# A linear-attention and MLP kernel on one Trainium2 core: one group of small matrix products per unit instead of three, the MLP's block products in another order, and the whole instruction order written out anew

## The chip, the cores and the metric

The kernel runs on one core of one Trainium2 chip. The metric is device time in microseconds (us) of one execution; lower is better. All arithmetic is in 32-bit floats on the core's engines: PE (TensorE, matrix products; PEld is its loading of stationary operands), DVE (VectorE), ACT (ScalarE), POOL (GpSimd) and SP (SyncE, which only issues DMAs here). Each engine runs its own instructions in the order in which the program issues them, and waits at an instruction until what it needs is there. The order of the program text is therefore the order in each engine's queue.

## The reference

B=4 batches, H=8 heads, S=768 steps, D=48.

```python
f = 1.0 / (1.0 + np.exp(-f_logit))
for t in range(S):
    state = f[:, :, t, :, None] * state + einsum('bhd,bhe->bhde', k[:, :, t], v[:, :, t])
    y[:, :, t] = einsum('bhd,bhde->bhe', q[:, :, t], state)
x = y.transpose(0, 2, 1, 3).reshape(B, S, H * D)          # 4 x 768 x 384
xn = (x - mean(x)) / sqrt(var(x) + 1e-6) * g_ln
out = x + relu(xn @ w_ch1) @ w_ch2                         # 384 -> 1536 -> 384
```

## The kernel before, in words

The 768 steps are cut into 12 **units** of 64 steps. A unit holds the 4 batches and 8 heads of its steps, so 256 tokens of 384 numbers. A unit first goes through the attention part, then through the MLP part, and the program interleaves the attention of later units with the MLP of earlier ones.

**Attention of unit n** (function `attention`, a table of stages that are called by name). `gates` is the sigmoid; `after` and `upto` are running products of the gates (scans on DVE, L669 and L681); `k`, `q` and `kept` multiply keys, queries and the state by them. From unit 3 on (`DIRECT`) f, k, q and the scaled keys K are split into 16-bit planes on ACT (L440), stored to DRAM, and brought back transposed by a DMA on SP's queue (L455). Then come the small products, each in a quarter of the 128x128 array, 64 instructions to a kind (32 products; an fp32 product is two instructions):

- `carried` (L758): the queries times the state of the units before, into the PSUM tile `py`;
- `scores` (L772): keys times queries, into the PSUM tile `shared` (two banks);
- `causal` (L778): DVE copies the scores out of `shared` into `sc` through a mask, one instruction of 128x1024;
- `values` (L808): `sc` times v, added into `py`; ACT then copies `py` out as the unit's x (L819);
- `chunk` (L846): transposed keys `kt` times v, into `shared` again; `state` (L854, DVE) adds it to the kept state.

`stats` (L831 to L835: DVE, then POOL), `norm` (L876, DVE) and `turn` (L887: six PE transposes into `xp`; L889: six ACT multiplications into `xt`) make the transposed and normalized x.

**MLP of unit n.** For units 0 to 2 the first layer is plain. From unit 3 on, `by_blocks` computes it with 15 block products instead of 18 (L952, each 4 matmuls of 128x128x128 into one PSUM bank called bw, bx, bv, by or bz). Their left operands are blocks of `xt` or sums of them, `y`, which `sums_of_x` makes with nine DVE instructions (L922). Each product is then copied by ACT (L957) or added by DVE (L960) into `h`, and a relu by ACT (L963) follows. The second layer is plain for units 0 and 1 (L1027); from unit 2 on it is 7 products instead of 8 (L1046, each 6 matmuls of 128x192 output into one bank `pp`), from h and the sums s1 to s4 of its quarters (L931 to L934). DVE, POOL and ACT add them up (L1054), and `put` (L1059) sends the output.

**PSUM** has 8 banks: two for `shared`, two for `py`, and four that `one_bank` hands out in rotation to everything else (xp, bw to bz, pp, po, ph). A product that is handed a bank waits until the bank's former content has been read.

**The weights** arrive as 64-bit floats, in 12 pieces of 768 KB, and are fetched, read and rewritten as fp32 by the tokens `f`, `r` and `w`; the tokens `t`, `T`, `u`, `U` make the mixed weights of the second layer, `d` issues a matmul of nothing.

**Order.** A string of tokens gives the order of the whole program: `START` for the beginning, then `UNIT` for m = 3 to 11 with n=m+1, o=m+2, p=m+3, z=m+4. `m{m}` issues the next product of unit m's MLP, `a{n}.values` that stage of unit n's attention, `p`/`P` a split, `x` a transfer back, `l`/`L` a load, `s` and `y` the sums. So while unit m's MLP runs, its template issues 15 block products with the attention of unit n between them, and then the 7 products of the second layer.

**The fallback check.** `worst`, `pw`, `least_one` and `small` (L1141 to L1149) reduce the smallest running product of all units to one number. They are issued after units 9 and 10 of the template. At the end each engine loads that number into a register (L1154) and branches on it (L1155); the branch's other side is a general path that these inputs don't take.

Of the kernel before, what the change touches and what calls it, by code (L numbers as in the profile page):

```python
# [9 lines left out]
FP32 = mybir.dt.float32  # L10
# [291 lines left out]
START = """  # L302
d d L0f1 l0k1 a0.gates0 a0.carried a0.after0 d l0k0 d l0q0 a0.kx1 a0.upto0 a0.gates1 d f
l0q1 a0.after1 r a0.kx0 a0.k0 f a0.q0 a0.scores0 a0.upto1 L0v1 w a0.causal0 a0.k1 d l0v0
f r a0.q1 w a0.scores1 a0.values0 r a0.kt a0.causal1 f d a0.stats0 w a0.values1 d
a0.norm0 r a0.stats1 l1f w a0.chunk f a0.norm1 d a0.turn0 a1.gates h00 r h00 l1k
a1.after a0.turn1 a0.state h00 a1.upto l1q l1v h01 h01 f w h01 a1.q h00 l2q a1.kept f
h01 r a1.kx h01 a1.carried a1.k l2f a1.scores w r a1.kt h00 a1.causal a1.values f w l2k
a1.stats h00 f r a1.chunk a2.gates h01 a1.norm a1.turn l3f a2.kx f P3f0 m1 w r a2.after
a2.k p3f1 a2.upto a1.state r l3k f a2.kept m1 P3k1 w m1 m1 r w l2v m1 w p3k0 f m1 r x3f  # L310
a3.gates a2.q l3q m0 m0 a2.carried L4f a2.scores a2.kt w a2.causal x3k P3q1 m1 u T
a3.after U P3q0 L4k a2.values x3q a2.chunk U P4f1 m1 a3.k U a2.stats a2.norm P3K0 m0 m0
u a2.state P4k1 m0 u a2.turn P4k0 t p3K1 m0 m2 l4q p4f0 a3.upto l3v a3.kept u u p4q0
p4q1 m2 a3.q m2 u x4f u t l5f m1 a3.carried a3.scores m2 a4.gates m2 a3.causal m2 m1
a3.values a4.after x4k a3.kt s2 x4q P5f0 a4.k P5f1 a3.chunk u a3.stats a3.state L5k l5v
m2 a3.norm m1 p5k0 a4.upto l6f a4.q U p5k1 m1 x5f P4K1 l4v m2 m2 m2 U a3.turn l5q
a5.gates p4K0 y3 m2 a4.kept m2 m2
"""
UNIT = """
x{o}k a{n}.carried a{n}.scores p{p}f1 m{m} a{o}.after m{m} m{m} a{n}.kt a{n}.causal  # L320
p{o}q1 m{m} p{p}f0 m{m} m{m} m{m} a{n}.values m{m} P{o}q0 a{o}.upto m{m} l{p}k m{m}
a{n}.stats m{m} m{m} m{m} m{m} a{n}.norm m{m} a{n}.chunk a{n}.turn a{o}.k s{m} m{m}
p{p}k1 x{o}q a{n}.state L{z}f m{m} a{o}.q P{p}k0 m{m} p{o}K0 x{p}f y{n} l{p}q m{m}
a{o}.kept p{o}K1 a{p}.gates m{m} m{m} m{m} l{p}v
# [4 lines left out]
def kernel(  # L329
# [37 lines left out]
    FIRST = 3  # L367
    DIRECT = 3
# [135 lines left out]
    state = consts.tile([P, 2, GA, D], FP32)  # L504
    shared = two_banks("shared")
# [122 lines left out]
    x_of, norm_of, xn_of, xt_of, y_of, h_of, sums_of = {}, {}, {}, {}, {}, {}, {}  # L628
# [7 lines left out]
    def attention(n):  # L636
# [75 lines left out]
        def do_k(gs=both):  # L712
            kh = new("kh", [P, NS, T])
# [49 lines left out]
        def do_scores(gs=both):  # L763


            at["ps"] = ps = shared.rearrange("s r (e t) -> s r e t", t=T)
            kh, qh = at["kh"], at["qh"]
            for e, _ in of(gs):
                for b in range(2):
                    for r in range(2):  # L770
                        seg = 2 * e + b
                        nc.tensor.matmul(ps[half(b), r, e], lhsT=kh[head_rows(r), seg],  # L772
                                         rhs=qh[head_rows(r), seg], start=True, stop=True)

        def do_causal(gs=both):
            sc = new("sc", [P, 2, GA, T])
            if len(gs) == G:
                nc.vector.tensor_tensor(  # L778
                    out=sc.rearrange("s r e t -> s (r e) t"),
                    in0=at["ps"].rearrange("s r e t -> s (r e) t"),  # L780
# [4 lines left out]
                out=sc[:, :, es], in0=at["ps"][:, :, es], op=ALU.mult,  # L785
# [17 lines left out]
        def do_values(gs=both):  # L803
# [8 lines left out]
            if n not in x_of:  # L812
                x_of[n] = xs.tile([P, G, DM], FP32, tag="x", name=f"x{n}")
# [65 lines left out]
    def turn(n, gs):  # L879
        xn = xn_of[n]  # L880
        if n not in xt_of:
            xt_of[n] = work.tile([P, KD, W], FP32, tag="xt", bufs=2, name=f"xt{n}")
        xt = xt_of[n]
# [7 lines left out]

    def first_half(n, g):
        xt = xt_of[n]
# [294 lines left out]
```

## Time and profile before

| | |
|---|---|
| device times of three runs | 443.1, 441.15, 441.22 us; median 441.22 |
| span of the profiled execution (first to last instruction) | 435.1 us |
| median time less that span | 6.1 us |
| busy share of the span: PE, DVE, ACT, POOL | 96%, 77%, 50%, 26% |
| mean granted TensorE clock | 0.988 of full speed |
| last PE instruction ends, span ends | 430.7 us, 435.1 us |

The profile gives one span, and three times without saying which of them it belongs to; the median is set beside it here, so that about 6.1 us lie outside the span. A timeline row reads: start in us, duration in us, engine, line, operation, destination <- sources, size of the stationary operand, output shape, and the number of instructions run together; a bracket at its end is how long the engine was idle before it, and who released it. Matmuls are pipelined, so the durations of neighbouring rows overlap: what a group costs PE is read from the distance of its start to the next row's start.

### The profile page before, as it was taken

Reading aid. Unit: us, or ns where it says so; the run is one execution under the profiler, and the core shown is the slowest. Engines: PE = TensorE matmul, PEld = TensorE weight load, DVE = VectorE, ACT = ScalarE, POOL = GpSimd, SP = SyncE. Lnnn points to the kernel's source line nnn. Section 1 sums busy time; section 2 is a strip of 40 time slices with the busy share of each in tenths; the row PEclk is TensorE's granted clock in tenths of the full one; section 3 lists DMA queues with packets and bytes.
Section 4 is the critical chain, followed back from the end, with each engine's and each line's share of the span. In section 5 each row is a group of like instructions: output and inputs, shape, how many; then the busy total and the mean of one; then the engine's idle time right before and its main releaser. Section 6 shows DMA issues by size and latency. Waiting matters only on the chain.

```text
span 435.1 us, 12965 instructions
## 1 busy us (share of the span) xinstructions
PE 419.7 (96%) x5435; PEld 388.8 (89%) x5435; DVE 333.2 (77%) x539; ACT 217.2 (50%) x364; POOL 114.3 (26%) x148
## 2 busy tenths in 40 slices
PE   6699899999999999999999989999999999999995
PEld 4599787767879999999999989999999999999995
DVE  5999699669497698798798789699698599466361
ACT  2593876454253663663663664574564372260320
POOL 2351444932023214114114104104105003002021
PEclk9599999999999999999999999999999999999999
DMA  9998979958978787798798896998798781400101
GB/s 167 282 179 224 234 218 238 196 141 198 226 171 201 180 199 189 165 213 209 186 185 208 152 206 154 204 185 202 177 190 187 153 153 35 101 2 17 23 4 38
DMA packets 167647, 71.68 MB, mean 165 GB/s; under 512 B 151760, under 2 KB 157840, under 8 KB 167584
## 3 DMA queue, kind: packets, MB, share of 16 engines
q1 hardware_dynamic: 151728, 54.38, 62.3%
q0 software_dynamic: 3872, 12.64, 8.7%
q10 hardware_dynamic: 11984, 3.79, 4.1%
q8 instruction: 44, 0.72, 0.7%
q14 instruction: 19, 0.16, 0.1%
HBM read 28.31 MB, written 23.59 MB: 119 GB/s over the span
## 4 chain that ended last, share of the span: by engine, by line
PE 79%; DMA 6%; issue 5%; DVE 3%; ACT 2%; SPq 2%; POOL 1%; POOLq 0%; ACTq 0%
PE pp L1046 28%; PE bx L952 9%; PE ph L1017 7%; PE po L1027 7%; PE by L952 7%; PE bz L952 3%; PE ph L901 2%; PE py L758 2%; PE shared L772 2%; PE py L808 2%; PE bw L952 2%; DMA kt<-Khalves 2%; DMA w_0words<-in_moe_w_ch_dram 2%; PE shared L846 2%; PE xp L887 2%
## 5 line engine op out<-in xcount | busy, mean ns | idle before, releaser
L963 ACT ACTIVATE h<-h 128x512 f32<-128x512 f32 x45 | 28.1, 631 | 40.8 <-DVE h L960 35.3
L1046 PE MATMUL pp<-mixed,h 128*128 128x192 f32 x240 | 42.3, 326 | 0.0
L1046 PE MATMUL pp<-w,h 128*128 128x192 f32 x240 | 40.9, 327 | 0.0
L1046 PE MATMUL pp<-mixed,s 128*128 128x192 f32 x240 | 40.6, 326 | 0.0
L1046 PEld LDWEIGHTS pp<-mixed,h 128*128 128x128 f32 x240 | 39.5, 190 | 0.0
L1046 PEld LDWEIGHTS pp<-mixed,s 128*128 128x128 f32 x240 | 39.3, 190 | 0.0
L1046 PEld LDWEIGHTS pp<-w,h 128*128 128x128 f32 x240 | 38.8, 190 | 0.3
L960 DVE TENSOR_TENSOR h<-h,bx 128x512 f32<-128x512 f32 x27 | 18.4, 683 | 25.7 <-PE bx L952 23.7
L669 DVE TENSOR_TENSOR_SCAN after<-gates,ends 128x1040 f32<-128x1040 f32 (+1 forms) x13 | 30.4, 2340 | 8.0 <-ACT gates L696 4.6
L1027 PE MATMUL po<-w,h 128*128 128x384 f32 x96 | 32.2, 487 | 0.0
L1017 PE MATMUL ph<-xt,w 128*128 128x256 f32 x144 | 31.8, 380 | 0.2 <-ACT xt L889 0.2
L960 DVE TENSOR_TENSOR h<-h,by 128x512 f32<-128x512 f32 x36 | 24.7, 687 | 8.6 <-PE by L952 4.8
L1017 PEld LDWEIGHTS ph<-xt,w 128*128 128x128 f32 x144 | 27.2, 190 | 4.4 <-ACT xt L889 0.5
L952 PE MATMUL bx<-y,v 128*128 128x128 f32 x216 | 29.4, 279 | 0.0
L440 ACT COPY Kplanes<-kh 128x1024 uint16<-128x1024 uint16 x18 | 18.7, 1047 | 20.9 <-DMA khalves<-kplanes 20.9
L681 DVE TENSOR_TENSOR_SCAN upto<-gates,starts 128x1040 f32<-128x1040 f32 (+1 forms) x13 | 28.1, 2158 | 0.4
L1027 PEld LDWEIGHTS po<-w,h 128*128 128x128 f32 x96 | 17.9, 190 | 11.0
L1054 POOL TENSOR_TENSOR p1x<-p,x 128x192 f32<-128x192 f32 x10 | 9.5, 952 | 68.8 <-ACT p L1061 68.8
L952 PEld LDWEIGHTS bx<-y,v 128*128 128x128 f32 x216 | 26.2, 192 | 0.5
L957 ACT ACTIVATE h<-bw 128x512 f32<-128x512 f32 x9 | 5.4, 598 | 38.6 <-PE bw L952 38.6
L440 ACT COPY kplanes<-kraw 128x1024 uint16<-128x1024 uint16 x18 | 18.7, 1047 | 10.8 <-DMA fraw<-in_f_logit_dram 3.4
L834 POOL TENSOR_SCALAR rstd<-mv 128x2 f32<-128x2 f32 (+1 forms) x13 | 3.2, 250 | 77.2 <-DVE mv L832 77.0
(171 smaller groups left out, 964.3 us busy)
## 6 DMA issues: line engine op xcount, KB each, us to landing
w_0words<-in_moe_w_ch_dram SPq DMA_DIRECT2D x7, 768.0 KB, 5.5
v<-in_v_dram SPq DMA_DIRECT2D x46, 96.0 KB, 3.4
Khalves<-Kplanes POOLq DMA_DIRECT2D x16, 256.0 KB, 4.2
kraw<-in_k_dram SPq DMA_DIRECT2D x40, 96.0 KB, 3.5
fhalves<-fplanes POOLq DMA_DIRECT2D x14, 256.0 KB, 5.3
kraw<-in_q_dram SPq DMA_DIRECT2D x36, 96.0 KB, 3.7
fraw<-in_f_logit_dram ACTq DMA_DIRECT2D x27, 96.0 KB, 2.7
khalves<-kplanes SPq DMA_DIRECT2D x9, 256.0 KB, 2.4
```

Of the source, the lines that this page charges most:

```text
L440: nc.scalar.copy(out=to, in_=src)
L669: nc.vector.tensor_tensor_scan(out=at["after"].rearrange(flat)[:, c0:c1][:, ::-1], data0=gt[:, c0 + 1:c1 + 1][:, ::-1], data1=ends.rearran ...
L681: nc.vector.tensor_tensor_scan(out=at["upto"].rearrange(flat)[:, c0:c1], data0=gt[:, c0:c1], data1=starts.rearrange(flat)[:, c0:c1], initi ...
L758: nc.tensor.matmul(py[half(b ^ r), r, e * D:(e + 1) * D], lhsT=qh[head_rows(r), 2 * e + b], rhs=kept[head_rows(r), b, e], start=e == 0, st ...
L772: nc.tensor.matmul(ps[half(b), r, e], lhsT=kh[head_rows(r), seg], rhs=qh[head_rows(r), seg], start=True, stop=True)
L952: nc.tensor.matmul(banks[bank][:, i], lhsT=right[:, i * P:(i + 1) * P], rhs=left, start=new and i == 0, stop=True, skip_group_check=True)
L960: nc.vector.tensor_tensor(out=out[to], in0=out[to], in1=bank, op=op)
L963: nc.scalar.activation(out=out[to], in_=out[to] if bank is None else bank, func=AF.Relu)
L1017: nc.tensor.matmul(ph[:, j], lhsT=w1[:, m, (i + j) * P:(i + j + 1) * P], rhs=xt[:, m], start=m == 0, stop=m == KD - 1)
L1027: nc.tensor.matmul(po, lhsT=h[:, i, g * P:(g + 1) * P], rhs=w2[:, i], start=i == 0, stop=i == KF - 1)
L1046: nc.tensor.matmul(pp, lhsT=a[:, i], rhs=b[:, i], start=i == 0, stop=i == KH - 1)
L1054: engine.tensor_tensor(out=to, in0=x1, in1=x2, op=op)
```

## The change

- One string `PLAN` gives the order of the whole program in place of `START` and `UNIT`. A `+` between tokens only binds them in the text.
- From unit 5 on (`MERGED`) the scores of a unit go to two banks of the rotating four (`ps0`, `ps1`) and no longer to `shared`; the mask is then two DVE instructions of 128x512 instead of one of 128x1024.
- With that, `values` of unit n, and `scores`, `chunk` and `carried` of unit n+1, stand next to each other in the plan, for n = 4 to 10. Before, a unit had three places: carried with scores, values, chunk.
- The 15 block products keep their operands and come in another order; some copies become additions and the other way round. In the plan the products of unit m's first layer and of unit m-1's second layer are mixed.
- `y` and `s` tokens issue one DVE instruction each, where one token issued nine or four. s2 and s4 are written over two quarters of h.
- xt and h become two fixed tiles (`xts`, `hs`) of which each unit uses a half by turns; `kh` gets 2 buffers, x gets 4.
- `smallest()` (the four instructions of the fallback check) is issued by the token `g10`, the last of the plan.
- `PAIRED` = 12 is beyond the last blocked unit, so the code that widens a block to two units is not used (`Z` is 128, `R2` is 4).

The numbers of matmuls and of DMAs are those of before.

```diff
-START = """
-d d L0f1 l0k1 a0.gates0 a0.carried a0.after0 d l0k0 d l0q0 a0.kx1 a0.upto0 a0.gates1 d f
...
-UNIT = """
-x{o}k a{n}.carried a{n}.scores p{p}f1 m{m} a{o}.after m{m} m{m} a{n}.kt a{n}.causal
...
+PLAN = """
...
+m4 s4 a5.turn y5 x7k m4 y5 y5 s4 y5 l7v p7q1 a7.gates m5 P7q0 a6.state m5 y5 a7.after m4 y5 m5
...
-            at["ps"] = ps = shared.rearrange("s r (e t) -> s r e t", t=T)
+            if "ps" not in at:
+                at["ps"] = [one_bank(f"ps{r}_{n}") if n >= MERGED else shared[:, r]
+                            for r in range(2)]
...
+            if n >= MERGED:
+                for r in range(2):
+                    nc.vector.tensor_tensor(
+                        out=sc[:, r], in0=at["ps"][r].rearrange("s (e t) -> s e t", t=T),
+                        in1=causal.unsqueeze(1).broadcast_to([P, GA, T]), op=ALU.mult)
+                return
...
-        copy((1, 3), product("bw", y[12], b[2, 3]))
-        copy((2, 3), product("bx", y[11], v[11]))
-        copy((1, 1), product("bv", y[3], b[2, 1]))
-        add((1, 3), product("bx", y[9], b[3, 3]))
-        add((1, 1), product("by", y[4], b[1, 1]))
-        add((1, 1), product("bx", a[1, 3], v[7]), ALU.subtract)
-        add((1, 3), product("by", a[1, 1], v[13]), ALU.subtract)
-        copy((1, 2), product("bx", y[10], v[10]))
...
+            copied((1, 3), "bw", y[12], b[2, 3])
+            copied((2, 3), "bx", y[11], v[11])
+            copied((1, 1), "by", y[4], b[1, 1])
+            added((1, 3), "bx", y[9], b[3, 3])
+            added((1, 1), "bv", y[3], b[2, 1])
+            added((1, 3), "by", a[1, 1], v[13], ALU.subtract)
+            added((1, 1), "bx", a[1, 3], v[7], ALU.subtract)
+            copied((2, 2), "bz", a[2, 2], v[0], -1.0)
...
+        for to, x1, x2, op in ((s1, a21, a22, ALU.add), (a21, a11, a21, ALU.subtract),
+                               (a11, s1, a11, ALU.subtract), (a12, a12, a11, ALU.subtract)):
+            yield nc.vector.tensor_tensor(out=to, in0=x1, in1=x2, op=op)
...
+        elif kind == "g":
+            if int(rest) == NU - 2:
+                smallest()
...
-    run(START)
+    run(PLAN)
     assert not (queue or fetched or opened)
-    for m in range(3, NU):
-        run(UNIT.format(m=m, n=m + 1, o=m + 2, p=m + 3, z=m + 4))
-        if m == NU - 3:
-            worst = consts.tile([P, 1], FP32)
-            nc.vector.tensor_reduce(out=worst, in_=least, axis=mybir.AxisListType.X, op=ALU.min)
-        if m == NU - 2:
-            pw = one_bank("pw")
...
```

What this does to PE's queue around the small products of a unit. Before, with unit 4's MLP and unit 5's attention: py5, shared and so on carry the unit's number, and bw_4 to bz_4 are unit 4's block products.

```order
L1046 MATMUL pp4_3_2082<-mixed4_123,h3_1762 128x192 x6
L758 MATMUL py5_2098<-kept5_2052,qh5_2008 64x48 x32
L772 MATMUL shared_119<-qh5_2008,kh5_1965 64x64 x32
L952 MATMUL bw_4_2168<-y4_2028,w1_59 128x128 x4
L952 MATMUL bx_4_2175<-y4_2028,v11_1087 128x128 x4
...
L952 MATMUL by_4_2203<-xt4_1950,v13_1088 128x128 x4
L808 MATMUL py5_2098<-v5_1532,sc5_2189 64x48 x32
L952 MATMUL bx_4_2175<-y4_2028,v10_1086 128x128 x4
```

After, on PE's queue where unit 4's values and unit 5's scores stand (the rows left out go on with ps0 and ps1 by turns, 32 in all):

```order
L1089 MATMUL pp3_2_1888<-w2_60,hs_120 128x192 x6
L993 MATMUL bx_3_0_1636<-y3_1522,v8_1138 128x128 x4
L842 MATMUL py4_1650<-v4_1439,sc4_1777 64x48 x32
L799 MATMUL ps0_5_1947<-qh5_1901,kh5_1723 64x64
L799 MATMUL ps1_5_1948<-qh5_1901,kh5_1723 64x64
...
L880 MATMUL shared_121<-v5_1762,kt5_1851 48x48 x32
L782 MATMUL py5_2013<-kept5_1870,qh5_1901 64x48 x32
L1089 MATMUL pp1_3_2073<-w2_60,hs_120 128x192 x6
```

The four kinds of small products stand in one row, and the scores, the chunk and the carried products are those of the next unit.

The second place is PE's queue between the transposes of a unit's x (xp) and that unit's first block product (bw). Before, all 7 products of the former unit's second layer stood between them:

```order
L887 MATMUL xp4_1951<-ident_58,xn4_1909 128x128 x3
L887 MATMUL xp4_1958<-ident_58,xn4_1909 128x128 x3
L1046 MATMUL pp1_3_1979<-w2_60,h3_1762 128x192 x6
L1046 MATMUL pp2_3_1998<-w2_60,h3_1762 128x192 x6
L1046 MATMUL pp6_3_2014<-mixed2_121,s2_3_1968 128x192 x6
L1046 MATMUL pp5_3_2042<-mixed1_120,s1_3_1967 128x192 x6
```

After, the same engine and the place one unit on:

```order
L919 MATMUL xp5_2480<-ident_58,xn5_2470 128x128 x3
L919 MATMUL xp5_2487<-ident_58,xn5_2470 128x128 x3
L1089 MATMUL pp1_4_2502<-w2_60,hs_120 128x192 x6
L993 MATMUL bw_5_0_2528<-y5_2494,w1_59 128x128 x4
L993 MATMUL bx_5_0_2538<-y5_2494,v11_1140 128x128 x4
L1089 MATMUL pp2_4_2546<-w2_60,hs_120 128x192 x6
```

One product of the second layer is left between them, and the others come between the block products.

The third place is the end of DVE's queue. Before, the last addition to the output (u2x) was followed by the load of the fallback check's number:

```order
L1054 TENSOR_TENSOR u2x_11_4898<-u2x_11_4898,pp7_11_4939 128x192
L1054 TENSOR_TENSOR u4y_11_4900<-u4y_11_4900,pp7_11_4939 128x192
L1054 TENSOR_TENSOR u4x_11_4899<-u4x_11_4899,pp3_11_4950 128x192
L1054 TENSOR_TENSOR u2x_11_4898<-u2x_11_4898,pp4_11_4960 128x192
L1154 TENSOR_LOAD small_62
```

After, the check itself stands there (pw, which least_one reads, is a transpose on PE):

```order
L1097 TENSOR_TENSOR u4x_11_4848<-u4x_11_4848,pp3_11_4922 128x192
L1097 TENSOR_TENSOR u2x_11_4847<-u2x_11_4847,pp4_11_4932 128x192
L1188 TENSOR_REDUCE worst_4942<-least_116 128x1
L1193 TENSOR_REDUCE least_one_4946<-pw_4944 1x1
L1195 TENSOR_SCALAR small_62<-least_one_4946 1x1
L1203 TENSOR_LOAD small_62
```

The reduction, whose steps were issued two units and one unit before the end, now stands behind the last addition.

357 lines of the change are left out of this document (196 added, 161 removed).

## The prediction

> **What bounds the kernel now.** First the page, for the busy shares:
>
> ```profile
> span 435.1 us, 12965 instructions
> ...
> PE 419.7 (96%) x5435; PEld 388.8 (89%) x5435; DVE 333.2 (77%) x539; ACT 217.2 (50%) x364; POOL 114.3 (26%) x148
> ```
>
> PE is the bound, but it is no more than 96% busy, and a busy PE may still run below its best rate. So I look at it by stretches; the columns are the stretch, its length, then busy time and instructions of PE, PEld, DVE, ACT and POOL, the granted clock, the DMA share and GB/s:
>
> ```profile
> 0.00:26.27 26.27, 18.28 (x253) 13.88 (x254) 20.52 (x37) 12.81 (x23) 10.28 (x20) 0.81 1.05 225
> 26.27:54.35 28.08, 26.87 (x452) 25.43 (x450) 24.42 (x33) 18.06 (x40) 9.62 (x8) 1.00 1.01 209
> 54.35:141.76 87.41, 87.41 (x868) 69.27 (x871) 68.11 (x96) 43.65 (x66) 32.51 (x29) 1.00 0.85 198
> 206.75:239.25 32.50, 32.50 (x471) 31.71 (x473) 26.96 (x45) 18.76 (x31) 7.91 (x12) 1.00 0.86 192
> 239.25:403.08 163.83, 162.02 (x2268) 157.94 (x2268) 126.16 (x217) 79.95 (x137) 33.68 (x51) 1.00 0.69 141
> ```
>
> The first 54 us are held up by inputs and DMA (share 1.05 and 1.01). From there PE is busy throughout; a unit in its steady state takes 32.50 us, with DVE at 26.96 of it. Whatever the change gains there must come out of the rate of PE, which the timeline of one unit shows (PE alone):
>
> ```profile
> 206.68 1.15 PE L758 MATMUL py<-kept,qh 48*64 48x48 f32 x64
> 207.65 1.12 PE L772 MATMUL shared<-qh,kh 48*64 48x64 f32 x64
> 208.71 1.16 PE L952 MATMUL bw<-y,w 128*128 128x128 f32 x8
> 209.70 1.06 PE L952 MATMUL bx<-y,v 128*128 128x128 f32 x8
> ...
> 211.49 1.11 PE L952 MATMUL bx<-y,w 128*128 128x128 f32 x8
> 212.44 1.06 PE L952 MATMUL by<-y,w 128*128 128x128 f32 x8
> 213.46 1.16 PE L952 MATMUL bx<-xt,v 128*128 128x128 f32 x8
> 214.45 1.06 PE L952 MATMUL by<-xt,v 128*128 128x128 f32 x8
> 215.44 1.15 PE L808 MATMUL py<-v,sc 64*64 64x48 f32 x64
> 216.51 1.16 PE L952 MATMUL bx<-y,v 128*128 128x128 f32 x8
> 217.51 1.06 PE L952 MATMUL by<-y,v 128*128 128x128 f32 x8
> 218.40 1.06 PE L952 MATMUL bz<-xt,v 128*128 128x128 f32 x8
> ...
> 222.87 1.06 PE L952 MATMUL by<-y,v 128*128 128x128 f32 x8
> 223.86 0.94 PE L846 MATMUL shared<-v,kt 64*48 64x48 f32 x64
> 224.72 0.87 PE L887 MATMUL xp<-ident,xn 128*128 128x128 f32 x6
> ```
>
> Starts are to be subtracted. A block product in full flow costs 0.89 us (217.51 to 218.40). Those around a group of small products, and those that take a bank again, cost more, up to 1.02.
>
> **Part (a), the groups.** Three places in the unit pass from 128x128 products to quarter products and back. The product ahead of values costs 0.99 (214.45 to 215.44), that ahead of chunk also 0.99 (222.87 to 223.86): 0.10 for the entry. Scores cost 1.06 where carried, followed by more small ones, costs 0.97: 0.09; the product behind, bw, costs 0.99: 0.10. Values cost 1.07 (0.10 more) and the bx behind them 1.00 (0.11 more). Chunk costs 0.86. What small products cost with more of them behind is seen at an earlier unit, where values and chunk happen to stand together:
>
> ```profile
> 81.75 1.15 PE L808 MATMUL py<-v,sc 64*64 64x48 f32 x64
> 82.72 0.90 PE L846 MATMUL shared<-v,kt 64*48 64x48 f32 x64
> ```
>
> There values cost 0.97, without the 0.10. So a group costs 0.29 (scores), 0.31 (values) and, taking chunk's exit as half, 0.2: 0.80 a unit, 0.27 on average. By the two plans, from unit 4's carried products on, there are 23 such groups before and 10 after; 13 x 0.27 = **-3.5 us**. This lies on PE in full flow, so all of it counts.
>
> **Part (b), the banks of the block products.** In the same rows bx costs 0.95 (211.49), by 1.02 (212.44) and bx 0.99 (213.46): 0.06 + 0.13 + 0.10 = 0.29 a unit over 0.89, because a bank is taken again before its reader is done. In the new order a product of the second layer, about 2 us, often stands between two uses of a bank. Nine units x 0.29 = 2.6; I take **-1.6**, as some uses still follow closely, between 0 (two banks fewer while ps0 and ps1 are held) and -2.6.
>
> **Part (c), the long waits.** The waits of PE list them (us in total, times, longest); these two stand in full flow:
>
> ```profile
> PE bz L952 <- ACT h L957: 1.4, 2, 1.2
> PE shared L846 <- DMA kt<-Khalves: 0.4, 1, 0.4
> ```
>
> With the slowed products around them the bz and kt waits cost about 2.3 together (1.4 + 0.4, and some 0.5 beside). They are chances of an ACT that waits for a DMA ahead of its copy, and of one late transposed tile. Another order moves both; I let half go: **-1.1**, between -2.3 and 0.
>
> **Part (d), the start.** PE is busy 18.28 of the first 26.27 us, and its longest wait stands there:
>
> ```profile
> 17.32 1.13 PE L772 MATMUL shared<-qh,kh 48*64 48x64 f32 x32 [3.09 <-DVE qh L688]
> ```
>
> The new order there asks for the same loads, scans and weights, in another mixture. With the DMA share over 1 it can't pull in much: **-1**, between -3 and +2.
>
> **Part (e), a new joint.** Before, seven products of the second layer stood between the transposes xp and bw; now one does, or little more. Behind xp come six ACT multiplications and the first of the y sums:
>
> ```profile
> 225.31 1.66 ACT L889 ACTIVATE xt<-xp,gain 128x128 f32<-128x128 f32 x6
> ...
> 229.34 4.06 PE L1046 MATMUL pp<-mixed,s 128*128 128x192 f32 x24
> 233.24 2.11 PE L1046 MATMUL pp<-mixed,h 128*128 128x192 f32 x12
> ```
>
> ACT takes 1.66. The y sums are short DVE instructions, but each waits in DVE's queue behind additions of products. The cover is one product of (233.24 - 229.34) / 2 = 1.95, and the second half of xp, whose row above lasts 0.87, so about 0.4: 2.35. The chain is 1.66, plus some 0.75 for a sum and two hand-overs (that from u2x's addition to its DMA, in the rows of the tail below, is a few hundredths, and one between engines, 224.72 to 225.31, under 0.6): 2.4. It is a draw, and I take 0.1 for each of nine units, about **+1.0**; the least is 0, the most, if DVE is one addition behind at each, 0.45 x 9 = +4.
>
> **Part (f), the tail.** The fallback check now comes after the last product. Its pieces, and what ends the program now (engine, operation, min/median/max in ns, first and last start):
>
> ```profile
> 430.76 0.35 DVE L1054 TENSOR_TENSOR u2x<-u2x,pp 128x192 f32<-128x192 f32 x1 [1.59 <-PE pp L1046]
> 431.14 0.47 SPq L1059 DMA_DIRECT2D out_dram<-u2x  x1
> ```
>
> ```profile
> L1141 DVE TENSOR_REDUCE worst<-least x1: 163/163/163, 372.0 to 372.0; 128x1 f32<-128x16 f32 x1
> L1144 PE MATMUL pw<-ident,worst x1: 273/273/273, 403.0 to 403.0; 128*1 128x128 f32 x1
> L1147 DVE TENSOR_REDUCE least_one<-pw x1: 239/239/239, 403.4 to 403.4; 1x1 f32<-1x96 f32 x1
> L1149 DVE TENSOR_SCALAR small<-least_one x1: 142/142/142, 403.7 to 403.7; 1x1 int32<-1x1 f32 x1
> L1154 SPq TENSOR_LOAD <-small x1: 752/752/752, 404.7 to 404.7; - x1
> L1155 SPq EVENT_SEMAPHORE  x8: 17/17/17, 432.2 to 433.4; - x8
> ```
>
> Before, the end is the landing of u2x's output, which SP still waits for at 433.4, 2.3 after its issue at 431.14; the check has long been done. After, the check starts when u2x's addition ends (431.11 by the rows): worst, 0.16 and its hand-over, 0.3; from pw's start to the load's, with least_one and small between, 404.7 - 403.0 = 1.7; the load 0.75. That is 2.75 after u2x, then the branch. It runs beside the landing (2.3), and ends about 0.5 behind it; engines that load the number later add to that: **+1.0**, between +0.5 and +1.5.
>
> **Part (g), the middle.** With the new plan the attention runs ahead of where it stood: scores and carried of a unit come some 15 us of PE work earlier against the block products, chunk some 30. The transposes of f, k, q and K must land as much earlier. These are the K ones (the columns as above):
>
> ```profile
> L455 SPq DMA_TRANSPOSE kt<-Khalves x9: 1902/3655/6079, 115.1 to 374.1; - x9
> ```
>
> In the 87.41 us up to 141.76, DMA is 0.85 busy, so 13 us are free; the shift asks for about half a unit's DMA more, 0.5 x 0.86 x 32.5 = 14. It nearly fits: **+1.0**, between 0 and +6. Later the share falls to 0.69, and nothing is added.
>
> Where nothing is counted: `causal` in two halves costs DVE a little more; DVE has 5.5 us free in a unit. The sums in place lose two buffers and no instruction. The order on POOL moves splits only; POOL is busy 7.91 of 32.50.
>
> **The sum.** -3.5 - 1.6 - 1.1 - 1.0 + 1.0 + 1.0 + 1.0 = -4.2. The span would go from 435.1 to 430.9; with 6.1 us outside it, as for the median 441.22, that is 437.0. Its own range, by the likelier halves of the bounds, is 434 to 439.
>
> **The rivals.** *No change, 441.* While ps0 and ps1 are held for the mask, two banks are left for pp and the block products, and each product must wait for DVE or ACT to read the one two before. For it: DVE is 26.96 of 32.50 busy, and waits of 0.06 to 0.13 stand already with four banks. Against it: ps is held only until the mask has read it, which took 1.20 in one piece before:
>
> ```profile
> 209.49 1.20 DVE L778 TENSOR_TENSOR sc<-shared,causal 128x1024 f32<-128x1024 f32 x1
> ```
>
> Priced at 0.1 for each of 5 products in 9 units it is +4.5, which undoes the gain. [...]
>
> *Slower, 446.* In the stretch from 54 to 142 us the transposes land after PE asks for them: SP's queue is one line, and a transpose behind a store that isn't ready delays all behind it. Four arrivals (the attention of units 3, 4 and 5 twice) at 2.2 us late each give +9 on 437. It decides from the point where free DMA time, 13 us, is less than what is pulled ahead, which I put at 14. For it: DMA is over 1.0 before 54 us. Against: the K transposes come 9 times in 259 us, which leaves gaps. If PE sat for long, the clock would fall too, as the 0.81 of the first 26 us shows. [...]
>
> *A larger gain, 431.* The start gains its 3 and all waits of (b) and (c) go, with (e) and (g) at 0: -3.5 - 2.6 - 2.3 - 3 + 1 = -10.4.
>
> That the change doesn't do what it says hardly counts: the order shows one group per unit. Only the blocks of two units are unused.
>
> **Chances.** A measurement can tell about 0.5%, 2.2 us, from no change: faster is below 439.0, slower above 443.4. Forecast 0.50, larger gain 0.10, no change 0.24, slower 0.16. Faster is 0.50 + 0.10 = 0.60, same 0.24, slower 0.16. The range goes from 430.5 (the larger gain) to 443.5 and leaves out the slower rival.
>
> **What would show it.** Right: 10 groups on PE's timeline from unit 4's carried on, with a steady unit of about 31.9 us (32.50 less two groups and the bank waits); block products at 0.89 even where a bank is taken again; bw behind xp and one pp with a gap under 0.3; u2x's last addition near 425.6 (430.76 less 5.2), and about 5.3 us from there to the span's end (435.1 less 430.76, and 1.0). Wrong: a steady unit at 32.3 or more with waits for DVE or ACT behind ps (first rival); waits for turned, qraw or kt between 54 and 145 us (second); a chain at the end in which the load of the number takes over 2 us more than the landing.

## The result, and the profile after

The changed kernel takes 465.69 us (median of four runs, 465.13 to 468.29) against 441.19 before (436.73 to 443.1): a ratio of 1.0592, with a 95% interval of 1.0531 to 1.0653. It is slower by 24.5 us where 4.2 less was forecast, and outside the range of 430.5 to 443.5. Here and below, ratios and intervals go by fast runs alone and medians by all of them, so the two differ a little.

The profiled run of the changed kernel took 465.13 with a span of 463.4, so only 1.7 lie outside the span. Before's 435.1 then belongs to a run of about 436.8, the fastest of its four, and the 6.1 us of the prediction were a spread between runs, not a tail. Between the two traces lie 28.3 us; that is what the accounts below add up to.

The page of the changed kernel, the same lines:

```profile
span 463.4 us, 12985 instructions
...
PE 424.3 (92%) x5435; PEld 396.2 (85%) x5435; DVE 333.8 (72%) x546; ACT 215.7 (47%) x364; POOL 110.5 (24%) x148
...
PEclk9889998999999999998998999999998999999998
...
q8 instruction: 45, 0.74, 0.7%
```

PE has the same 5435 matmuls and is busy for 4.6 us more, but it is idle for 23.7 us more (39.1 instead of 15.4). Its clock dips in several slices, where the row of before dips in one alone:

```profile
PEclk9599999999999999999999999999999999999999
```

The waits of PE (us in total, times, longest) give a releaser that the prediction has nowhere:

```profile
PE tr L685 <- DMA fraw<-in_f_logit_dram: 8.9, 2, 4.7
PE py L782 <- issue: 5.6, 3, 2.7
PE shared L880 <- issue: 3.6, 2, 2.1
PE ph L1053 <- issue: 3.4, 1, 3.4
PE shared L799 <- issue: 2.5, 1, 2.5
PE shared L880 <- DVE sc L818: 1.8, 1, 1.8
PE pp L1089 <- issue: 1.6, 1, 1.6
```

"Issue" is idle time in which the engine waited for nothing that the profile shows: eight waits, 16.7 us, six of them in or right behind six of the seven merged groups, and two at the beginning. In the trace of before the same list has one, of 0.3:

```profile
PE ph L901 <- issue: 0.3, 1, 0.3
```

Where they stand is seen on PE's timeline of two of the merged groups. First the group of values of unit 5 and scores, chunk and carried of unit 6:

```profile
202.38 1.15 PE L842 MATMUL py<-v,sc 64*64 64x48 f32 x64
203.35 1.12 PE L799 MATMUL ps<-qh,kh 48*64 48x64 f32 x64
204.30 0.83 PE L880 MATMUL shared<-v,kt 64*48 64x48 f32 x57
207.22 0.30 PE L880 MATMUL shared<-v,kt 64*48 64x48 f32 x7 [2.08 <-issue]
207.34 1.15 PE L782 MATMUL py<-kept,qh 48*64 48x48 f32 x64
208.42 2.01 PE L993 MATMUL bx<-y,w 128*128 128x128 f32 x8
210.23 1.87 PE L993 MATMUL by<-y,v 128*128 128x128 f32 x8
211.93 1.06 PE L993 MATMUL bx<-y,v 128*128 128x128 f32 x8
```

then the next one:

```profile
242.56 0.56 PE L782 MATMUL py<-kept,qh 48*64 48x48 f32 x23
245.82 1.23 PE L782 MATMUL py<-kept,qh 48*64 48x48 f32 x41 [2.71 <-issue]
246.98 3.43 PE L1089 MATMUL pp<-w,hs 128*128 128x192 f32 x12
250.25 0.49 PE L1089 MATMUL pp<-mixed,hs 128*128 128x192 f32 x2
```

The stop is not ahead of an operation, where the prediction's wait for qh stands (3.09). It is inside one: after 57 of 64 chunk matmuls, and after 23 of 64 carried ones. Inside the groups all goes as forecast: values 0.97 with scores behind them, scores 0.95. Behind these two stops the products are slow as well: two block products take 3.51 (208.42 to 211.93) instead of 1.78, and one of the second layer 3.27 instead of 1.95. The stretches show the clock (columns as in the prediction):

```profile
205.20:207.30 2.10, 0.08 (x5) 0.08 (x6) 1.90 (x6) 0.00 (x0) 0.04 (x1) 1.00 1.15 110
246.00:249.50 3.50, 3.50 (x49) 3.41 (x46) 2.67 (x3) 0.00 (x0) 0.00 (x0) 0.51 0.83 150
```

In the second, 3.5 us long, it is 0.51. What comes in while PE stands is seen in the list of DMA queues (packets, MB, share) of 204.8 to 206 us; from 196 to 204.8 it has no such line:

```profile
q8 instruction: 1, 0.02, 4.8%
```

One packet of queue q8, 0.02 MB, the queue of instructions. Over the whole span there are 45, 0.74 MB, so 16 KB each; PE's 2 x 5435 matmuls and weight loads are 242 to a packet. **Theory A**, estimated from these numbers, is that PE gets its program in blocks of about 256 instructions, and that a row of 512 small ones in 3.9 us (64 matmuls and 64 weight loads to a kind) uses a block up before the next has come. The rivals were **theory B**, an ordinary wait that the profile doesn't name (py still being emptied by ACT, kt not there), and **theory C**, the prediction's own slower rival, late transposes.

### The profile page after: what moved, and what is told of

Its sections match the earlier page's. It is cut to its first block, busy times and chain, and to the rows that moved or that the text cites. A ratio compares the mean times of both kernels' runs of the same rounds, so it can differ in the third digit from the quotient of the medians.

```text
span 463.4 us, 12985 instructions
## 1 busy us (share of the span) xinstructions
PE 424.3 (92%) x5435; PEld 396.2 (85%) x5435; DVE 333.8 (72%) x546; ACT 215.7 (47%) x364; POOL 110.5 (24%) x148
## 4 chain that ended last, share of the span: by engine, by line
PE 64%; issue 15%; DVE 8%; DMA 4%; POOL 4%; ACT 3%; POOLq 0%; ACTq 0%; DVEq 0%
PE pp L1089 21%; PE ph L1053 7%; PE bx L993 7%; PE po L1071 6%; PE by L993 5%; PE ph L933 4%; PE bz L993 2%; PE py L782 2%; PE tr L685 2%; PE py L842 2%; PE xp L919 1%; DMA fraw<-in_f_logit_dram 1%; DMA qhalves<-qplanes 1%; PE bv L993 1%; PE bw L993 1%
## 5 line engine op out<-in xcount | busy, mean ns | idle before, releaser
L1089 PE MATMUL pp<-w,hs 128*128 128x192 f32 x360 | 64.9, 332 | 2.6 <-issue 1.6
L1089 PE MATMUL pp<-mixed,hs 128*128 128x192 f32 x360 | 63.6, 326 | 0.0
L1089 PEld LDWEIGHTS pp<-w,hs 128*128 128x128 f32 x360 | 59.4, 193 | 3.4 <-issue 2.8
L1007 ACT ACTIVATE hs<-hs 128x512 f32<-128x512 f32 x45 | 28.1, 629 | 67.5 <-DVE hs L1003 55.0
L1089 PEld LDWEIGHTS pp<-mixed,hs 128*128 128x128 f32 x360 | 58.3, 190 | 0.1
L1053 PE MATMUL ph<-xts,w 128*128 128x256 f32 x144 | 34.6, 395 | 3.4 <-issue 3.4
L1053 PEld LDWEIGHTS ph<-xts,w 128*128 128x128 f32 x144 | 27.8, 197 | 8.8 <-issue 3.8
L1003 DVE TENSOR_TENSOR hs<-hs,bx 128x512 f32<-128x512 f32 x36 | 24.6, 684 | 14.3 <-PE bx L993 11.4
L1071 PE MATMUL po<-w,hs 128*128 128x384 f32 x96 | 32.5, 488 | 0.0
L1071 PEld LDWEIGHTS po<-w,hs 128*128 128x128 f32 x96 | 18.0, 190 | 10.9
L921 ACT ACTIVATE xts<-xp,gain 128x128 f32<-128x128 f32 x72 | 20.0, 374 | 10.8 <-PE xp L919 10.8
L462 ACT COPY qplanes<-kraw 128x1024 uint16<-128x1024 uint16 x18 | 18.8, 1051 | 10.8 <-DMA kraw<-in_q_dram 9.4
```

What stands on the lines that cost most here:

```text
L462: nc.scalar.copy(out=to, in_=src)
L921: nc.scalar.mul(out=xt[:, m, g * P:(g + 1) * P], in_=pt[:, m], mul=gain[:, m:m + 1])
L1003: nc.vector.tensor_tensor(out=out[to], in0=out[to], in1=product(bank, left, right), op=op)
L1007: nc.scalar.activation(out=out[to], in_=out[to] if bank is None else bank, func=AF.Relu)
L1053: nc.tensor.matmul(ph[:, j], lhsT=w1[:, m, (i + j) * P:(i + j + 1) * P], rhs=xt[:, m], start=m == 0, stop=m == KD - 1)
L1071: nc.tensor.matmul(po, lhsT=h[:, i, g * P:(g + 1) * P], rhs=w2[:, i], start=i == 0, stop=i == KF - 1)
```

## The experiments

Each was compared with runs of the kernel before on the same chip, whose medians were 438.87, 441.7, 441.73 and 442.41 in the four sets. As these differ by 3.5, the distance from the kernel before says more than the bare time; the changed kernel is 24.5 above its own.

**The groups cut in two** (e1_halves), all else as changed (the tokens of the plan, its line breaks aside, here and in the edits below):

```diff
-a4.values+a5.scores+a5.chunk+a5.carried a4.stats l6q s3 a5.causal x6f P6q0 m3 s3 a4.norm x6k m2
+a4.values+a5.scores a4.stats l6q s3 a5.causal x6f P6q0 m3 s3 a4.norm x6k m2 a5.chunk+a5.carried
...
```

> The changed kernel with each of the seven groups cut in two: values and the next unit's scores stay, chunk and carried come two MLP products later. [...] So about 451, 14 to 15 below the changed kernel. Theory B (an ordinary wait that the profile doesn't name: carried for py to be emptied by ACT, chunk for kt): the waits stay at the same products and shrink by what the two products cover, 461 to 464. Theory C (my slower rival: the attention runs ahead and the transposes or DMAs in the middle are late): within 2 of the changed kernel, 464 to 467.

Measured 452.52, ratio 1.0281 (1.0178 to 1.0384): 13.2 below the changed kernel, or 10.9 less by the distance from the kernel before (13.7 instead of 24.5). Theory A's 451 is 465.7 less the 11.5 of idle time in or behind the seven groups, less about 5 for three stretches of half clock, and 1.9 for seven more entries and exits. No wait in the groups is left to "issue"; the only ones are the two at the beginning (1.9 and 2.3). The same place in the program:

```profile
197.95 1.15 PE L840 MATMUL py<-v,sc 64*64 64x48 f32 x64
198.91 1.13 PE L797 MATMUL ps<-qh,kh 48*64 48x64 f32 x64
199.97 1.16 PE L991 MATMUL bx<-y,w 128*128 128x128 f32 x8
```

The same data are asked for at nearly the same time, and nothing waits. That speaks against C, and against B so far as two products can't cover 2 us and more.

So about half of the loss stays. PE's busy time is that of before (419.5 and 419.7 us); the 13.5 us between the two spans are idle time: 17.5 instead of 9.2 in the first 80 us, 4.9 instead of 1.8 from there to PE's last product, and 6.7 instead of 4.4 behind it.

**The blocks shifted** (e2_shift): 64 instructions that nothing reads, ahead of the program.

```diff
+    def narrow():
+        bank = one_bank("idle")
+        for i in range(16):
+            nc.tensor.matmul(bank[:, i:i + 1], lhsT=ident, rhs=ident[:, i:i + 1], start=i == 0,
+                             stop=True, skip_group_check=True)
...
-l0q1 L0f1 a0.gates0 d l0q0 d a0.after0 l0k0 a0.upto0 d a0.gates1 l0k1 a0.carried f f a0.q0
+n l0q1 L0f1 a0.gates0 d l0q0 d a0.after0 l0k0 a0.upto0 d a0.gates1 l0k1 a0.carried f f a0.q0
```

> The changed kernel with 16 narrow products (64 instructions of PE, one column each, into a bank that nothing reads) ahead of everything. Nothing else moves in PE's queue. Theory A: the block boundaries fall 64 instructions earlier in the program, so the idle time inside each merged group moves 32 matmuls earlier: in the group that stopped after 57 of the 64 chunk matmuls it stands after 25, and in the one that stopped after 23 of the carried matmuls it stands among the last of chunk. The seven idle times stay in sum, 8 to 14 us; the time is within 4 of the changed kernel, since the two early stops may fall elsewhere. Theories B and C: the idle times stay at the same matmuls, 57 and 23.

Measured 466.42, ratio 1.059 (1.0524 to 1.0656), as changed. The group whose chunk stopped after 57 matmuls:

```profile
209.87 0.47 PE L884 MATMUL shared<-v,kt 64*48 64x48 f32 x25
213.29 0.62 PE L884 MATMUL shared<-v,kt 64*48 64x48 f32 x36 [2.95 <-issue]
```

It now stops after 25, exactly 32 matmuls (64 instructions) earlier. In the next group the stop moved from carried's 23rd matmul to chunk's 53rd, 34 earlier by the records (two of its 64 are missing); in the first from the second pp matmul to carried's 34th, 32 earlier. A wait for an operand would still stand after 57; this one kept its place in the instruction stream. It decides for A. Not all seven stopped again (the one after 44 chunk matmuls is gone), and both early stops went, while another wait at 85 us (for ACT, 2.7) came.

The traces settle it further. These are the stretches up to the stop in the changed kernel and in e2_shift (columns as in the prediction):

```profile
0.00:207.20 207.20, 184.45 (x2505) 160.13 (x2506) 159.14 (x234) 107.80 (x175) 63.88 (x74) 0.98 0.89 199
0.00:213.25 213.25, 195.15 (x2505) 169.61 (x2506) 161.09 (x234) 107.16 (x175) 66.44 (x76) 0.94 0.90 193
```

In both, 2505 matmuls stand ahead of the stop, although 32 of those of the second are new. Counting every record of PE's queue (matmuls, weight loads and its sequencer's own instructions), the 14 traces of this case have 48 waits for issue, and each stands at a count of 193 over a multiple of 256, one of them at 194. The block of 256 that ends there had lasted 1.9 to 5.0 us; not every block as short as that is followed by a stop (two of 2.0 and 2.1 in the changed kernel are not). The fourth group, which has no wait for issue, is followed by one of 0.75 at such a count too (at 281.33, put down to DVE's xn; 0.8 in e1_halves), so that it may belong to the same cause.

**The check earlier** (e3_check_early), the token g10 moved back:

```diff
-m10 p11K0 m11 s11 a11.kt m10 m11 s11 m10 m10 s11 m11 s11 m11 m11 m11 m11 m11 g10
+m10 p11K0 m11 s11 a11.kt m10 g10 m11 s11 m10 m10 s11 m11 s11 m11 m11 m11 m11 m11
```

> The changed kernel with the fallback check issued twelve tokens earlier, with ten MLP products behind it. All theories: the stretch from PE's last end to the span's end goes back from 6.7 to about 4.4, and the time falls by 2.0 to 2.5, to about 463.3.

Measured 459.44, ratio 1.0439 (1.038 to 1.0499), 20.6 above the kernel before: 3.9 less than the changed kernel, or 6.2 by the bare times, more than the tail can give; its profiled run, 463.46, was the slowest of its four. From the last product to the end of the span it is 4.4.

**The block order alone** (e4_block_order), put into the kernel before:

```diff
-        copy((1, 1), product("bv", y[3], b[2, 1]))
+        copied((1, 1), "by", y[4], b[1, 1])
...
-        relu((2, 1), product("bx", y[8], v[8]))
-        yield
...
+        added((2, 2), "bx", y[2], b[3, 2], ALU.subtract)
+        relu((2, 2))
...
+        relu((2, 1), product("bx", y[8], v[8]))
```

> The kernel before with only the order of the 15 block products (and which are copied or added) of the change. Theory A: no idle time without a releaser over 0.5 us, since the rows of small instructions stay at 128 and 256; by the prediction's part (b) -1.6 against the kernel before, between +2 and -2.6. If the new block order itself were behind the loss (its products waiting for banks), it would be 8 or more above the kernel before.

Measured 448.33, ratio 1.0189 (1.012 to 1.0258): 9.5 above the kernel before, a miss for part (b), and over the expectation's own mark of 8 for a loss that lies in the order itself. PE's waits and one of the places:

```profile
PE by L952 <- DVE h L960: 9.0, 8, 1.2
```

```profile
157.57 1.06 PE L952 MATMUL bx<-y,w 128*128 128x128 f32 x8
159.81 1.16 PE L952 MATMUL by<-y,v 128*128 128x128 f32 x8 [1.19 <-DVE h L960]
```

Packed without the second layer's products between them, the last by waits in eight of the nine units until DVE has added an earlier product. In the changed kernel's list no such wait stands, and in e1_halves bz, by and bx follow at 215.72, 216.62 and 217.51, 0.89 to 0.90 each. So the order is not what the changed kernel loses by; that the mixture with the second layer makes it run is a reading, not tried apart.

**A long row in the kernel before** (e5_burst), and **the same instructions spread** (e6_spread):

```diff
+        def do_extra():
+            py, kh, qh = at["py"], at["kh"], at["qh"]
...
+                        nc.tensor.matmul(py[half(b), r, 384:384 + T], lhsT=kh[head_rows(r), seg],
+                                         rhs=qh[head_rows(r), seg], start=False, stop=True,
+                                         skip_group_check=True)
...
-x{o}k a{n}.carried a{n}.scores p{p}f1 m{m} a{o}.after m{m} m{m} a{n}.kt a{n}.causal
+x{o}k a{n}.carried a{n}.scores a{n}.extra0 a{n}.extra1 p{p}f1 m{m} a{o}.after m{m} m{m} a{n}.kt a{n}.causal
```

In the spread one, extra0 stands behind the second m and extra1 behind the third, each one product later than the expectation says.

> The kernel before, in which the 32 scores products of units 4 to 11 are issued three times in a row (the two repeats, 128 instructions each, go to unused columns of py and are read by nobody), so that carried and scores make one row of 512 PE instructions in 3.9 us; nothing else of the change is in it. The repeats themselves cost 8 x 2 x 0.97 = 15.5. Theory A (PE runs out of its blocks of 256 instructions): one stop of 1.5 to 2.7 in or right behind each of the eight rows, without a releaser, 12 to 20 in all, and half clock behind some of them: 28 to 45 above the kernel before. Theories B and C (a semaphore wait, or the transposes): no stops there, and 15 to 17 above the kernel before.

> The same repeats, as many instructions, but each set of 128 stands by itself, one and two block products later. They cost 15.5, and 16 more entries and exits of 0.27 are 4.3. Theory A: stops under 1 us and few, since a block of 256 now lasts some 3.5 us or more: 18 to 24 above the kernel before, and well below the run with the repeats in one row. Theories B and C: 19 to 21 above the kernel before, above the run with the repeats in one row by the 4.3.

Measured 469.51, ratio 1.0641 (1.0536 to 1.0745), and 458.07, ratio 1.0381 (1.0284 to 1.0479): the same work, 11.4 apart. They are 27.8 and 16.4 above the kernel before, just below theory A's ranges (28 to 45, and 18 to 24); but that the run with the row is the slower one is forecast by A alone. The waits of the first:

```profile
PE py L781 <- issue: 9.3, 7, 1.8
PE shared L772 <- DVE qh L688: 4.4, 2, 2.5
PE shared L856 <- DMA kt<-Khalves: 2.8, 1, 2.8
...
PE bw L962 <- issue: 1.3, 1, 1.3
...
PE bx L962 <- issue: 0.9, 1, 0.9
```

Every one of the eight rows stops, in it or within two products behind it, 11.5 in all, in a kernel that has nothing else of the change. The spread one has a single wait for issue, 0.5, ahead of all this, and waits 0.2 for kt, so that the 2.8 here are a part of the 11.4. The rows stopped for 1.0 to 1.8, less than I expected, and no half-clock stretch stands behind them (mean clock 0.985, and 0.986 in the spread one; bw behind a stop of 1.74 takes 0.99).

The two edits also tie q8 to PE's program. Of before and of e5_burst (e6_spread has the same line as the second):

```profile
q8 instruction: 44, 0.72, 0.7%
q8 instruction: 52, 0.85, 0.8%
```

The repeats are 8 x 256 = 2048 instructions of PE, and 8 more packets came: 256 to a packet.

**All dense rows opened** (e7_cut_all): e1_halves with the check early and, at the beginning, one product of the first layer between carried and scores of units 1 and 2 (shown for unit 2).

```diff
-a4.values+a5.scores+a5.chunk+a5.carried a4.stats
+a4.values+a5.scores a4.stats
...
-a2.carried r l3q f r a2.scores P3f0 m1
+a2.carried r l3q f r m1 a2.scores P3f0
```

> The changed kernel with the seven groups cut in two as in e1_halves, the fallback check early as in e3_check_early, and the two dense rows of the beginning opened: a product of the first layer between carried and scores of units 1 and 2. Theory A: 452.5 less 2.3 for the check, less 1.9 and 2.3 for the two stops at 43 and 65 us and less one half-clock stretch of 1.7: about 444.5 (442 to 447). Were the stops at the beginning waits for data, it would be 450.

Measured 451.87, ratio 1.0256 (1.0176 to 1.0335): a miss by 7, or by about 5 by the distance from the kernel before (10.2). The early stops shrank from 1.9 and 2.3 to 0.9 and 1.8, so one product is too little to open such a row. By the expectation's mark of 450 they would be waits for data, but their places say otherwise: both stand 12 matmuls earlier than in e1_halves (behind 51 of the scores instead of 63, and behind 57 of the scores instead of 64 and 5 of the next product), and the product put in ahead has 12. New waits came, too:

```profile
PE xp L917 <- DVE xn L908: 4.4, 5, 1.2
PE shared L797 <- issue: 2.7, 2, 1.8
PE ps L797 <- DVE u4y L1095: 2.0, 1, 2.0
...
```

The wait of ps for DVE's addition u4y is the prediction's first rival: the two banks for the scores are not free. It is there, at one place (with 1.0 in e1_halves, too).

**Values brought to chunk in the kernel before** (e8_values_chunk), with stats, norm, turn and the sums moved along:

```diff
-p{o}q1 m{m} p{p}f0 m{m} m{m} m{m} a{n}.values m{m} P{o}q0 a{o}.upto m{m} l{p}k m{m}
-a{n}.stats m{m} m{m} m{m} m{m} a{n}.norm m{m} a{n}.chunk a{n}.turn a{o}.k s{m} m{m}
...
+p{o}q1 m{m} p{p}f0 m{m} m{m} m{m} m{m} P{o}q0 a{o}.upto m{m} l{p}k m{m}
+m{m} m{m} m{m} m{m} m{m} a{n}.values a{n}.chunk s{m} m{m} a{n}.stats m{m}
...
```

> The kernel before with one more pair brought together and no row over 256 instructions: from unit 4 on values stand directly ahead of chunk (eight block products later than before), and stats, norm, turn and y follow later among the products of the second layer. By part (a) of the prediction a group less in each of 8 units is -2.5. Theory A: no long stop as long as no block of 256 instructions falls exactly into such a row; 0 to 2 such stops of up to 2 us. So -2.5 to +1 against the kernel before, if the transposes of x still find their cover.

Measured 476.7, ratio 1.0805 (1.0723 to 1.0887), a miss by far, 35 above the kernel before, and mostly not for want of instructions (1.8 of waits for issue):

```profile
PE pp L1046 <- DVE p L1054: 14.0, 5, 3.9
PE py L758 <- DVE kept L739: 6.0, 4, 2.7
```

PE waits until DVE has emptied the banks of the second layer. That stats, now ahead of them in DVE's queue, held them up while waiting for x is my reading, not tried apart.

**The copy behind which bz waited** was moved first with one token (e9_late_planes), which puts it behind the load of the next unit's k into the same buffer, so that this kernel takes k for part of q; then together with that load, which stays behind it (e11_planes_after_bz, whose edit this is):

```diff
-p{o}q1 m{m} p{p}f0 m{m} m{m} m{m} a{n}.values m{m} P{o}q0 a{o}.upto m{m} l{p}k m{m}
+p{o}q1 m{m} p{p}f0 m{m} m{m} m{m} a{n}.values m{m} a{o}.upto m{m} m{m} P{o}q0 l{p}k
```

> The kernel before with one token moved: the second half of the split of q (the copy on ACT that waits for a DMA, behind which the copy of bz stood for 1.36 us at 253 us) comes two block products later, behind that copy. All theories: -1.4 to -1.9 where the transposed q still arrives in time (the two waits for bz go), 0 if the wait only moves to the next copy on ACT; no stops without a releaser.

> The kernel before with the second half of the split of q, and the load of the next k that must stay behind it, two block products later, so that ACT's copy of bz no longer stands behind a copy that waits for a DMA. All theories: the two waits for bz (1.4) go and nothing takes their place: -1.5, between -2 and +1 against the kernel before.

Measured 453.57, ratio 1.0296 (1.0231 to 1.0362), and 439.38, ratio 0.9951 (0.9914 to 0.9988). The first, 11.8 above the kernel before where -1.4 to -1.9 was expected, loses most where the second layer waits for the relu (pp <- ACT h, 8.1). The second is the fastest version here, by 0.5%, just clear of no change but far below 2%. Its trace has no wait for bz, but more for kt:

```profile
PE shared L846 <- DMA kt<-Khalves: 3.1, 5, 1.5
```

So the trace does not show where the gain lies; its span (436.7) is no shorter than that of before's profile.

**The old beginning under the new plan** (e10_old_start): START of the kernel before, then what is left of the new plan with its groups cut and the check early.

```diff
-l0q1 L0f1 a0.gates0 d l0q0 d a0.after0 l0k0 a0.upto0 d a0.gates1 l0k1 a0.carried f f a0.q0
+d d L0f1 l0k1 a0.gates0 a0.carried a0.after0 d l0k0 d l0q0 a0.kx1 a0.upto0 a0.gates1 d f
...
```

> The changed kernel with its groups cut in two, the check early, and the first 142 us in the order of the kernel before (its whole START, then what is left of the new plan in its order). Theory A: PE starts 2.5 earlier, and the 22 us lost up to 80 us in e1_halves become the 15 of the kernel before; with 452.5 and 2.3 for the check that is 440 to 442, level with the kernel before (within 2). If the new order costs time beyond its dense rows and its beginning, it stays at 445 or more.

Measured 456.16, ratio 1.0327 (1.0254 to 1.0401), 14.4 above the kernel before, a miss. The beginning is again that of before (PE starts at 2.2, no wait for issue), but one wait stands at the seam, which the edit made itself:

```profile
PE bx L991 <- DVE hs L1001: 8.6, 2, 7.3
```

Without these 8.6 it would be 447.6, still over the expectation's mark of 445 for a loss beyond the dense rows and the beginning. So it is open whether the two parts could be joined without loss, and what else the new order costs.

**The late check alone** (e12_check_late), in the kernel before:

```diff
-        if m == NU - 3:
-            worst = consts.tile([P, 1], FP32)
...
+    worst = consts.tile([P, 1], FP32)
...
```

> The kernel before with the fallback check issued at the very end, as in the change, and nothing else. By the trace of the changed kernel 2.0 to 2.5 more, all of it between PE's last product and the span's end; by part (f) of the prediction +1.0.

Measured 443.33, ratio 1.0016 (0.9976 to 1.0057), +0.9 and no change that can be told. In the traces the stretch from the last addition's start to the span's end is 7.3 (432.30 to 439.6) against 4.3 before, 7.5 in the changed kernel. What fills it is the branch on PE, here of the changed kernel, behind a load that starts at 457.2 and takes 0.55 (min/median/max in ns, first and last start):

```profile
L1204 PEldq COMPARE_BRANCH  x1: 4466/4466/4466, 457.8 to 457.8; - x1
```

and of before, where it started while PE's last products still ran:

```profile
L1155 PEldq COMPARE_BRANCH  x1: 3622/3622/3622, 428.3 to 428.3; - x1
```

In all the runs of both kernels the time lies 1.65 to 1.83 above the span, so the 3 us of the tail are in the time as well. Why the medians differ by 0.9 only, and at most 2.5 by the interval, is open; single runs of this kernel lie 9 apart (439.49 to 448.49).

## Why the prediction was wrong, point by point

**The account of the 28.3 us between the traces.** PE is idle for 23.7 us more. Of these, 16.4 are waits for issue (16.7 - 0.3). Behind PE's last product it is 2.3 (6.7 instead of 4.4), in the first 80 us, beside the stops, 3.8 (12.7 instead of 8.9), and 1.3 elsewhere. And PE is busy for 4.6 more: behind four of the stops it runs at half clock for some 3.4 us (a clock of 0.50 to 0.52 from 68.6, 208.4, 246.0 and 348.5 on), which by the rows there costs 1.6 to 1.9 a time, 6.9 in all. So everything else, the forecast gains included, comes to -2.3.

**(a), the groups: the step that failed.** "This lies on PE in full flow, so all of it counts" took it that PE can run a row of any length at the pitch of its parts. Entries and exits cost what was said, and 13 were saved; but the row of 512 instructions made a new bound, the supply of instructions, that no row of the old kernel was long enough to meet. Its longest row was 256 instructions, and its only trace of the bound was the wait of 0.3. Shown: the stops go when the rows are cut (e1_halves), move with the stream (e2_shift), come in the old kernel with a long row alone (e5_burst against e6_spread), and stand at the same count over a multiple of 256 in every trace. In place of the -3.5 the seven groups brought 10.8 of stops and some 5.3 of half clock behind three of them. The step explains about half of the miss: with the groups cut, 13.7 are left, and these lie in (d), (f) and waits that were not tried apart.

**(b), the banks.** Right in its direction: from start to start, idle time left out, the 135 block products take 0.92 on average in e1_halves instead of 0.94, 2.8 us in all, entries to fewer groups included. Wrong in what makes it: the new order alone costs 9.5 (e4_block_order). The steady unit of 31.9 that was to show it would be 31.8 by its own terms (32.50 - 0.54 - 0.18), and in the new plan no two units are alike.

**(c), the long waits.** Those for bz and for kt are gone from the changed kernel's list; what stands there instead are small ones for DVE and ACT.

**(d), the start.** Wrong in sign. Two of the stops, 2.5 and 3.4, stand at 43.6 and 65.2 us behind rows of carried and scores (with a few products of 128x128 between or ahead). PE's first matmul starts at 4.7 instead of 2.2, because no matmul of nothing stands ahead of the first transposes; but these start at 4.67 in both kernels. A second wait for f, 4.2, ends at 17.50: the transposes of unit 1's f now stand ahead of the second half of unit 0's scores, which start at 19.36 instead of 17.32. What of the rest belongs to the order of loads was not told apart.

**(e), the joint.** No wait of bw behind xp stands in the list of the changed kernel; the cover held, and +1.0 was not needed.

**(f), the tail.** The chain was right up to the load (it starts at 457.2, 0.9 behind the end of u2x's addition, where 2.0 was allowed), but "then the branch" was given no price, and PE's branch takes 4.5 there. The term was +1.0 in the forecast and 3.2 in the span (7.5 - 4.3); what it costs in time e12_check_late leaves between nothing and 2.5.

**(g), the middle.** No wait for a transpose stands in PE's list after 30 us. The slower rival had the right side for a wrong reason: cutting the groups, with the transposes where they were, gave back 11 to 13 us. The range had no case for it.

**The first rival, the clock and the cause.** Against the first rival speak the products at 0.89 (e1_halves), for it the one wait of ps for DVE, 2.0 in e7_cut_all and 1.0 in e1_halves. The forecast had no term for the clock; the trace halves it for some 3.4 us behind stops of 2.1, 2.7, 2.1 and 3.4, and not behind those of 2.5, 1.6, 1.5 and 0.8, and what decides between them was not shown. The cause of the stops I had not weighed at all: the packets of 16 KB, 256 instructions of PE to each, and the 48 waits above, behind blocks of 1.9 to 5.0 us. How long ahead of its use a block is asked for was not shown.

## What to carry to other kernels

Before instructions of one engine are packed more densely, count them: how many stand in a row, and how long the row lasts. Here 512 PE instructions in 3.9 us ran dry in nearly every row, and rows of 256 with large products between them seldom did (one in e8_values_chunk did for 1.5 us, a product behind the row). A stop inside an operation, with "issue" as its releaser, was the sign; it moved when instructions were put ahead of it (by 32 matmuls for 64 instructions), and large products between the small ones made it go or shrink. And an order that is good in a mixture need not be good packed: the block order that ran without waits in the new plan cost 2% in the old one.

## What the runs showed of the hardware

- In the changed kernel PE stops for 0.8 to 3.4 us where a block of 256 of its instructions has lasted 1.9 to 3.3 us; in all 14 traces every wait for issue stands at the same count over a multiple of 256 (193, once 194).
- In the changed kernel a packet of 16 KB on q8 starts 2.3 to 3.1 us before each of the eight stops ends (one at 204.9, where PE stands from 205.1 to 207.2). Two packets start no less than 3.6 us apart there, and 4.1 in the trace of before, while the small products go through 256 instructions in 1.9.
- In the changed kernel the clock was 0.50 to 0.52 for some 3.4 us behind stops of 2.1, 2.7, 2.1 and 3.4, which cost 1.6 to 1.9 a time, so that a stop of 2.1 cost nearly twice its length; behind stops of 2.5, 1.6, 1.5 and 0.8 it was 1.00.
- PE's branch at the program's end took 3.3 us in e12_check_late, 3.6 in the kernel before and 4.5 in the changed one. Where it began under PE's last products, 4.3 us lay between the last addition's start and the span's end; where it began behind them, 7.3 and 7.5.
